# Mixing a chunk of 256 and one of 512 tokens, in place of three of 256, on each block of weights

## Chip, core and metric

The kernel runs on one core of a Trainium2 chip. The metric is the time of one execution on the device in microseconds, the median of several runs. TensorE does the matmuls, VectorE, ScalarE and GpSimd the rest, and SyncE (SP) issues most of the transfers.

## What is computed

Three layers follow each other: attention within clusters, a mixture of experts, and a bilinear layer. The change lies in the last, which the program calls the second stage:

```
def _moe2_ref(x, w_a, w_b, w_out) -> np.ndarray:
    a = x @ w_a
    b = x @ w_b
    return (a * b @ w_out).astype(np.float32)
```

x has 1536 tokens of 512 numbers. w_a and w_b are 512 x 1536, w_out is 1536 x 512. The weights come as 64-bit floats. The experts' outputs, which are x, go to a buffer ys_d in DRAM, sorted by expert, and come back from it in chunks of tokens.

## The kernel before

To hold its precision, the kernel splits each factor of a product into a high and a low part in the type fp32r, and makes a product of three matmuls (high by high, low by high, high by low). `mm3` issues these for a list of weight and token tiles: with four pieces of 128 rows (j = 0 to 3) that is 12 matmuls, first the two with the tokens' high part for each j, then those with the low part.

The second stage goes by steps I. One step has one chunk of tokens and one of 12 blocks of 128 columns of w_a and w_b. `bil1` multiplies the chunk by both blocks (24 matmuls), ScalarE copies the first result out of PSUM (L1311), VectorE multiplies it by the second (L1312), and ScalarE and VectorE split the product g into its two parts (L1313, L1317). `bil2` multiplies g by the block's rows of w_out, one or two steps later, and adds up in PSUM over the 12 blocks: three matmuls of 512 columns for each 128 tokens. At a chunk's end `leave` scales the sums by the gates and sends them out.

The order of steps is a list. Before, the first 36 steps mix three chunks of 256 tokens: on each four blocks of weights come four steps of chunk 0, four of chunk 1 and four of chunk 2. Then 12 steps take a chunk of 512 tokens and 12 a chunk of 256. A step of 256 tokens is called narrow here, one of 512 wide. A matmul of `bil1` has as many columns as the chunk has tokens.

While the first chunks are mixed, the weights of later blocks are still being loaded and narrowed from 64-bit floats, one piece of 128 x 512 in a step: `narrow_a` (ScalarE, L1053), `narrow_b` (VectorE, L1065 to L1067), `narrow_c` (ScalarE, L1073) and `narrow_d` (VectorE, L1079). The raw pieces stand in four buffers; the load of a piece four further on goes out when `narrow_b` is done with the buffer.

A chunk's tokens are loaded by `load_x2`, at the step that the table X2 gives, and split into high and low part by `split_x2` (ScalarE L1281, VectorE L1282), at the step that X2S gives. Steps below zero lie in the experts' stage. The outputs of the last expert, in the tile ys_7, are put into ys_d by `put_rows` (L1257) at step 2, behind that step's `load_x2`. The rows that it writes come from a register.

Engines take their instructions in the order in which the program issues them. Tiles that share a tag share its buffers: "xe" has two, which hold ys_6 and ys_7 when the second stage begins, and "xT" has two. The eight PSUM banks are sc0 to sc3, pp, pv, et0 and et1.

Of the kernel before, what the change touches and what calls it, by code (L numbers as in the profile page):

```python
# [9 lines left out]
F32 = mybir.dt.float32  # L10
F32R = mybir.dt.float32r
# [11 lines left out]
P = 128  # L23
FAR = float(2.0 ** 100)
CAP = 256
# [4 lines left out]
NA = 5  # L30
RAMP0, RAMP = 8, 3
GR = 5
CHUNKS = ((0, 256), (256, 256), (512, 256), (768, 512), (1280, 256))
X2 = {-7: 0, 0: 1, 4: 2, 27: 3, 39: 4}
X2S = {-3: [(0, 0), (0, 1)], 2: [(1, 0), (1, 1)], 6: [(2, 0), (2, 1)], 29: [(3, 0)], 31: [(3, 1)], 42: [(4, 0)], 43: [(4, 1)]}
I0 = 0
PACE = (1,)
YW = 1
CG0 = 2
LEAD = 24  # L40
# [7 lines left out]
def kernel(  # L48
# [15 lines left out]
    nc = tc.nc  # L64
# [12 lines left out]
    DC = DM // P  # L77
# [6 lines left out]
    rawp = ctx.enter_context(tc.tile_pool(name="rawp", bufs=NRAW))  # L84
# [13 lines left out]
    ys_v = ys_d.rearrange("(j p) n -> p j n", p=P)  # L98
# [21 lines left out]
    wide = w_a.dtype == I64  # L120
# [9 lines left out]
    raw = {}  # L130
    raw2 = {}
    hl = {}
# [675 lines left out]
    for s in range(nst):  # L808
        g_, h, t = steps[s]
        pp = g_[0]  # L810
# [149 lines left out]
    big = ctx.enter_context(tc.tile_pool(name="big", bufs=1, reuse_waits="tile"))  # L960
    xT_t = {}

    def new_x(key, dt=F32R):
        return big.tile([P, 2, DC, CAP], dt, tag="xT", name=f"xT_{key}", bufs=2)
# [82 lines left out]
    def narrow_a(m):  # L1047
        for _ in range(min(m, 4 * NCH - nsplit[0])):
            load_raw()
            w, hi, lo = open_part()  # L1050
            if w.dtype == I32:
                a = big.tile([P, 512], F32, tag="a", name=f"a_{nsplit[0]}", bufs=NA)
                nc.scalar.activation(a, w[:, :, 1].bitcast(F32), AF.Abs, scale=2.0 ** -112)  # L1053
                narrowed.append((w, a, hi, lo))
            else:
                nc.scalar.copy(hi, w)
                nc.gpsimd.tensor_sub(lo, w, hi)
            ndone[0] += 1
            load_raw()

    def narrow_b(m):
        for _ in range(min(m, len(narrowed))):
            w, a, hi, lo = narrowed.pop(0)
            low, top, au = w[:, :, 0].bitcast(U32), w[:, :, 1].bitcast(U32), a.bitcast(U32)
            nc.vector.tensor_scalar(out=au, in0=au, scalar1=3, scalar2=None, op0=ALU.logical_shift_left)  # L1065
            nc.vector.scalar_tensor_tensor(out=au, in0=low, scalar=29, in1=au, op0=ALU.logical_shift_right, op1=ALU.bitwise_or)
            nc.vector.scalar_tensor_tensor(out=au, in0=top, scalar=0x80000000, in1=au, op0=ALU.bitwise_and, op1=ALU.bitwise_or)  # L1067
            late.append((a, hi, lo))
# [7 lines left out]
    def narrow_d():  # L1076
        while lows:
            a, hi, lo = lows.pop(0)
            nc.vector.tensor_sub(lo, a, hi)  # L1079
# [34 lines left out]
    def mm3(ps, pairs):  # L1114

        ops = [o for (sh, sl_), (mh, ml) in pairs for o in ((sh, mh), (sl_, mh))]
        ops += [(sh, ml) for (sh, _), (_, ml) in pairs]
        for i, (s_, m_) in enumerate(ops):
            nc.tensor.matmul(ps, s_, m_, start=(i == 0), stop=(i == len(ops) - 1))  # L1119
# [51 lines left out]
    LAG = 2  # L1171
# [87 lines left out]

    NF2 = F2 // P  # L1260
    HD = DC // 2

    def load_x2(ck):

        at, wd = CHUNKS[ck]
        if ck == 2:
            x = [big.tile([P, DC, CAP], F32R, tag="xe", name=f"x2{n}_{ck}", bufs=2) for n in "hl"]
            x = [[x[m][:, HD * u:HD * u + HD] for u in range(2)] for m in range(2)]
        elif wd == CAP:
            x = new_x(f"b{ck}")  # L1270
            x = [[x[:, m, HD * u:HD * u + HD] for u in range(2)] for m in range(2)]
        else:
            x = [[rawp.tile([P, HD, wd], F32R, tag="raw", name=f"x2_{ck}{m}{u}") for u in range(2)] for m in range(2)]
        for u in range(2):
            nc.sync.dma_start(out=x[1][u].bitcast(F32), in_=ys_v[:, HD * u:HD * u + HD, at:at + wd])
        xT_t["b", ck] = x

    def split_x2(ck, u):

        hi, lo = (x[u] for x in xT_t["b", ck])  # L1280
        nc.scalar.copy(hi, lo.bitcast(F32))  # L1281
        nc.vector.tensor_sub(lo, lo.bitcast(F32), hi)  # L1282

# [1 line left out]
    outs = []  # L1285
    o_ps = {}
    o_f = {}
    banks = [("sc0", "sc1"), ("sc2", "sc3"), ("pp", "pv"), ("sc0", "sc1", "sc2", "sc3"), ("sc0", "sc1")]

    def bil1(I):  # L1290
        ck, f = order[I]
        c, ff = divmod(f, 4)
        at, wd = CHUNKS[ck]
        xh, xl = xT_t["b", ck]
        if wd == CAP:
            pab = ps_t.tile([P, 2, CAP], F32, tag=f"et{I % 2}", name=f"ab_{I}")
            pab = pab[:, 0, :], pab[:, 1, :]
        else:
            pab = [ps_t.tile([P, wd], F32, tag=t, name=f"ab{z}_{I}") for z, t in enumerate((("et0", "et1"), ("pp", "pv"))[I % 2])]
        for z in range(2):  # L1300
            w = hl[NCE + 3 * c + z]
            mm3(pab[z], [((w[:, 0, j, ff * P:(ff + 1) * P], w[:, 1, j, ff * P:(ff + 1) * P]), (xh[j // HD][:, j % HD, :], xl[j // HD][:, j % HD, :])) for j in range(DC)])
        narrow_a(PACE[I % len(PACE)] > 0 if I >= I0 else 0)
        if wd == CAP:
            ga = big.tile([P, CAP], F32, tag="ga", name=f"ga_{I}", bufs=2)
            g2 = big.tile([P, 2, CAP], F32R, tag="hh", name=f"g_{I}", bufs=4)
            gh, gl = g2[:, 0], g2[:, 1]
        else:
            ga = big.tile([P, wd], F32, tag="a", name=f"ga_{I}", bufs=NA)
            gh, gl = (big.tile([P, wd], F32R, tag="hh", name=f"g{m}_{I}", bufs=4) for m in range(2))  # L1310
        nc.scalar.copy(ga, pab[0])  # L1311
        nc.vector.tensor_mul(ga, pab[1], ga)  # L1312
        nc.scalar.copy(gh, ga)  # L1313
        narrow_c()
        narrow_a(PACE[I % len(PACE)] > 1 if I >= I0 else 0)
        narrow_b(1)
        nc.vector.tensor_sub(gl, ga, gh)  # L1317
        narrow_b(1)
        narrow_d()
        gs_[I] = (gh, gl)  # L1320

    def leave(ck, t):
# [32 lines left out]
                leave(ck, t)  # L1355


    order = [(ck, 4 * c + ff) for c in range(NF2 // 4) for ck in range(3) for ff in range(4)]
    order += [(ck, f) for ck in (3, 4) for f in range(NF2)]
    after = {J + LAG: [J] for J in range(len(order))}  # L1360
    w0 = 3 * NF2
    after.update({w0 + 1: [w0], w0: [w0 - 2, w0 - 1], w0 + NF2 + 1: []})
    after.update({J + 1: [J] for J in range(w0, w0 + NF2)})
    tot = len(order)
    pg_ = put_gates(lambda: gs_[max(gs_)][0])
    for G in range(total_f + tot + LAG):
        I = G - total_f

        skip_whole()
        room = 4 * (NSLOT + 2 * (max(G - LAG, 0) // 4)) - nsplit[0]  # L1370
        if 4 * NCE <= nsplit[0] and I < 0 and G % NF > 1:
            narrow_a(min(room, 1))
        if G == 1:
            ranks()
        if G == 2:
            limits()
        if G == GR:
            rare()
        if I < 0:
            layer1(G)  # L1380
            if G in (2, NF - 1):
                load_xe(1 if G == 2 else 2)
            if G == NF:
                further()
            if G == GR - 2:
                tc.mark_branch_hint_location("rare", "LikelyTaken", engines=[mybir.EngineType.DVE])
            e, f = divmod(G, NF)
            if 2 * NF <= G < 3 * NF:
                next(rr, None)
            if G > 3 * NF:  # L1390
                next(gg, None)
            if f == (5 if e else NF - 2):
                if e + 1 < NE:
                    trans_x(e + 1, xe_t[e + 1])
            if f == 5 and 0 < e < NE - 2:
                load_xe(e + 2)
        elif I < tot:
            bil1(I)
            next(pg_, None)
        if I in X2:  # L1400
            load_x2(X2[I])
        for ck, u in X2S.get(I, ()):
            split_x2(ck, u)
        if I >= LAG:
            for J in after[I]:
                bil2(J)
        elif G >= LAG:
            layer2(G - LAG)
        put_rows(G - LAG)
        if 3 <= G < total_f:  # L1410
            load_whole(G)
        if nsplit[0] < 4 * NCE:

            ramp = RAMP0 + 2 * min(G, GR - 2) + RAMP * max(G - GR + 1, 0)
            split_some(min(room, 2 * G + lead - nsplit[0], ramp - nsplit[0], 4 * NCE - nsplit[0]))
        elif I < 0:
            narrow_c()
            narrow_b(1)
            narrow_d()
        if G == GR - 1:  # L1420
            tc.mark_branch_hint_location("rare", "LikelyTaken", engines=[mybir.EngineType.SP])
# [30 lines left out]
```

## Time and profile before

| | |
|---|---|
| time, median of 3 runs | 779.07 us (778.71 to 779.94) |
| the profiled execution | 778.49 us |
| its span, first to last instruction | 776.4 us |
| TensorE busy | 754.8 us, 97% |
| VectorE busy | 462.6 us, 60% |
| ScalarE busy | 378.4 us, 49% |
| step 0 of the second stage begins | 464.67 us |
| the first wide step (step 36) begins | 617.44 us |
| the first step of the last chunk (step 48) begins | 716.30 us |

Times within an execution count from the first instruction of the span. A matmul's end is modelled and overlaps the next one's start, so a stretch of matmuls is measured from one start to another.

### The profile page before, as it was taken

The page shows a single profiled execution, that of the slowest core. Times are in us where ns is not written, and L with a number is a line of the kernel's source. Part 1 is how long each engine was busy: PE and PEld are TensorE (multiplying, and loading weights), DVE is VectorE, ACT ScalarE, POOL GpSimd, SP SyncE. Part 2 cuts the span into 40 slices and gives each one's busy share as a digit, 9 for nine tenths or more (in the row PEclk, how much of TensorE's full clock was granted, in tenths as well). Part 3 has the DMA queues.
Part 4 walks back from the last instruction along what each step waited for, and adds up shares of the span by engine and source line. Part 5 has one row for each costly group of instructions (what it writes and reads, how often), then busy time and mean ns, then how long its engine had stood idle before and what let it go on. Part 6 is the DMA issues. An engine that isn't in the chain of part 4 may idle for free.

```text
span 776.4 us, 13347 instructions
## 1 busy us (share of the span) xinstructions
PE 754.8 (97%) x5097; PEld 648.5 (84%) x5097; DVE 462.6 (60%) x929; ACT 378.4 (49%) x794; POOL 106.1 (14%) x143
## 2 busy tenths in 40 slices
PE   8899999999999988999999999999999999999996
PEld 5667777777777668999999999999999988888995
DVE  6776665787767776378876898877743221121211
ACT  5656766667675665266654555544423211111211
POOL 6203212051300041000000004420001110000201
PEclk9999999999999999999999999999999999999999
DMA  7228133152221026789879866773401000000100
GB/s 187 60 80 270 45 94 87 59 182 96 60 52 32 28 96 225 271 299 296 276 243 275 280 218 186 154 139 113 136 1 55 28 28 1 0 1 1 55 1 27
DMA packets 48519, 91.91 MB, mean 118 GB/s; under 512 B 6328, under 2 KB 21304, under 8 KB 48448
## 3 DMA queue, kind: packets, MB, share of 16 engines
q1 hardware_dynamic: 44240, 81.01, 35.8%
q0 software_dynamic: 2304, 6.31, 2.1%
q10 hardware_dynamic: 1904, 3.67, 1.3%
q8 instruction: 41, 0.67, 0.3%
q14 instruction: 30, 0.25, 0.1%
HBM read 69.27 MB, written 14.04 MB: 107 GB/s over the span
## 4 chain that ended last, share of the span: by engine, by line
PE 32%; issue 22%; DVE 2%; DMA 2%; POOL 1%; ACT 1%; POOLq 0%; DVEq 0%; ACTq 0%
PE ab L1119 11%; PE y L1236 4%; PE o_sc L1352 4%; PE h L1201 3%; PE y L1240 2%; PE h L1119 2%; PE h L1193 2%; DMA raw<-in_moe_w_dram 2%; PE h L1202 1%; DVE w L207 1%; PE y L1241 1%; POOL out_dram L1330 1%; PE o_pp L1352 1%; PE o_pv L1352 1%; PE xT L1100 0%
## 5 line engine op out<-in xcount | busy, mean ns | idle before, releaser
L1312 DVE TENSOR_TENSOR ga<-ab,ga 128x256 f32<-128x256 f32 (+1 forms) x60 | 28.6, 477 | 156.0 <-ACT ga L1311 84.8
L564 ACT ACTIVATE E<-sc,nmx 128x768 f32<-128x768 f32 x96 | 86.8, 904 | 56.3 <-DVE nmx L559 47.3
L1119 PEld LDWEIGHTS ab<-xT_b,w 128*128 128x128 f32 x864 | 107.8, 191 | 2.6
L1119 PE MATMUL ab<-xT_b,w 128*128 128x256 f32 x864 | 109.2, 283 | 0.0
L559 DVE TENSOR_REDUCE nmx<-sc 128x1 f32<-128x768 f32 x96 | 91.4, 953 | 17.1 <-PE sc L551 16.0
L1311 ACT COPY ga<-ab 128x256 f32<-128x256 f32 (+1 forms) x60 | 25.0, 417 | 151.9 <-PE ab L1119 151.9
L579 PEld LDWEIGHTS et<-ident,E 128*128 128x128 f32 x576 | 62.6, 141 | 34.7 <-ACT ET L583 12.5
L1352 PE MATMUL o_sc<-w,g 128*128 128x512 f32 x360 | 90.1, 392 | 0.0
L579 PE MATMUL et<-ident,E 128*128 128x128 f32 x576 | 82.2, 279 | 4.8 <-ACT E L564 2.8
L585 DVE COPY ET<-et 128x384 f32<-128x384 f32 x96 | 52.6, 548 | 54.9 <-PE et L579 54.8
L1352 PEld LDWEIGHTS o_sc<-w,g 128*128 128x128 f32 x360 | 65.4, 189 | 12.1
L606 PE MATMUL pv<-ET,v 128*64 128x384 f32 (+2 forms) x408 | 73.0, 479 | 0.6 <-ACT ET L583 0.5
L550 PE MATMUL sc<-K,Q 80*128 80x512 f32 x192 | 72.8, 380 | 0.5 <-DMA Q<-Q 0.5
L207 DVE TENSOR_TENSOR w<-raw,w 128x1024 fp32r<-128x1024 f32 x48 | 58.2, 1219 | 17.2 <-ACT w L206 16.6
L1119 PE MATMUL ab<-x,w 128*128 128x512 f32 x288 | 67.7, 391 | 0.2 <-DVE ot L1329 0.2
L1119 PEld LDWEIGHTS ab<-x,w 128*128 128x128 f32 x288 | 54.0, 188 | 12.1 <-DVE ot L1329 0.6
L551 PE MATMUL sc<-K,Q 128*128 128x512 f32 x192 | 61.7, 342 | 0.0
L1236 PE MATMUL y<-hh,w 128*128 128x256 f32 (+3 forms) x416 | 59.4, 290 | 0.8 <-issue 0.8
L206 ACT CAST w<-raw 128x1024 fp32r<-128x1024 f32 x48 | 50.3, 1051 | 16.1 <-DMA raw<-in_moe_w_dram 11.1
L1313 ACT CAST g<-ga 128x256 fp32r<-128x256 f32 (+1 forms) x60 | 26.9, 449 | 59.7 <-DVE ga L1312 59.7
L1236 PEld LDWEIGHTS y<-hh,w 128*128 128x128 f32 x416 | 54.5, 190 | 1.2 <-issue 0.9
L583 ACT COPY ET<-et 128x384 f32<-128x384 f32 x96 | 45.7, 476 | 2.7 <-PE et L579 2.6
(272 smaller groups left out, 1253.9 us busy)
## 6 DMA issues: line engine op xcount, KB each, us to landing
raw<-in_moe_w_dram SPq DMA_DIRECT2D x48, 512.0 KB, 5.1
w<-in_moe_w_dram SPq DMA_DIRECT2D x16, 512.0 KB, 6.6
raw<-in_moe_w_a_dram SPq DMA_DIRECT2D x12, 512.0 KB, 4.5
raw<-in_moe_w_b_dram SPq DMA_DIRECT2D x12, 512.0 KB, 4.8
raw<-in_moe_w_out_dram SPq DMA_DIRECT2D x12, 512.0 KB, 5.2
xs_d<-zero SPq DMA_DIRECT2D x8, 512.0 KB, 6.2
xe<-xs_d ACTq DMA_DIRECT2D x7, 512.0 KB, 7.2
v<-in_v_dram SPq DMA_DIRECT2D x8, 384.0 KB, 3.1
```

The costliest lines, as they stand in the source:

```text
L206: nc.scalar.copy(hi, w)
L207: nc.vector.tensor_sub(lo, w, hi)
L550: nc.tensor.matmul(ps[:, lo:hi], Q3[:, qs], K3[:, h * S + lo:h * S + hi], start=True, stop=False)
L551: nc.tensor.matmul(ps[:, lo:hi], Q2[:, qs], K2[:, h * S + lo:h * S + hi], start=False, stop=True)
L559: nc.vector.tensor_reduce(out=nmx[pp][:, h, t:t + 1], in_=sc[s], axis=AX.X, op=ALU.max, negate=True)
L564: nc.scalar.activation(e, sc.pop(s), AF.Exp, bias=nmx[pp][:, h, t:t + 1], accum_out=sums[pp][:, t, h:h + 1])
L579: nc.tensor.transpose(pt[:, j * P:(j + 1) * P], e[:, kt * P:(kt + 1) * P], ident)
L585: nc.vector.tensor_copy(dst, src)
L606: nc.tensor.matmul(pv[h * D:(h + 1) * D, :], vt[:, h, kt, :], ets[g, h][:, kt, :n * P], start=(kt == 0), stop=(kt == NT - 1))
L1119: nc.tensor.matmul(ps, s_, m_, start=(i == 0), stop=(i == len(ops) - 1))
L1236: nc.tensor.matmul(ys_ps[e][j // 2][:, j % 2, :wd], w[:, m_, ff, j * P:(j + 1) * P], s_, start=(f == 0 and i == 0 and j % 2 == 0), stop=(l ...
L1352: nc.tensor.matmul(o_ps[ck][t], s_[:, t * P:(t + 1) * P], w_[:, m_], start=(f == 0 and i == 0), stop=(J == I and f == NF2 - 1 and i == 2))
```

## The change

Chunks 1 and 2, of 256 tokens each, become one chunk of 512. The mixed part then has 24 steps: on each four blocks of weights four narrow steps of chunk 0 and four wide steps of chunk 1. The chunks behind it stay, under new numbers (2 and 3).

The 512 tokens of chunk 1 stand in two halves: j = 0, 1 in a tile of tag xT, j = 2, 3 in two tiles of tag xe. `load_x2` loads a half at a time, so X2 has entries for halves. A wide step narrows a second piece at its end. Wide steps have their results in et0 and et1 alone, where they had taken turns with pp and pv; chunk 0 adds up in pp and pv, chunk 1 in sc0 to sc3. When a step's `bil2` runs is worked out by a loop: after the next step for a wide one, two steps later for a narrow one.

```diff
-CHUNKS = ((0, 256), (256, 256), (512, 256), (768, 512), (1280, 256))
-X2 = {-7: 0, 0: 1, 4: 2, 27: 3, 39: 4}
-X2S = {-3: [(0, 0), (0, 1)], 2: [(1, 0), (1, 1)], 6: [(2, 0), (2, 1)], 29: [(3, 0)], 31: [(3, 1)], 42: [(4, 0)], 43: [(4, 1)]}
+CHUNKS = ((0, 256), (256, 512), (768, 512), (1280, 256))
+X2 = {-7: [(0, 0), (0, 1)], 0: [(1, 0)], 2: [(1, 1)], 19: [(2, 0), (2, 1)], 27: [(3, 0), (3, 1)]}
+X2S = {-3: [(0, 0), (0, 1)], 2: [(1, 0)], 3: [(1, 1)], 20: [(2, 0)], 21: [(2, 1)], 30: [(3, 0)], 31: [(3, 1)]}
...
-    def load_x2(ck):
+    x2_t = {}
+
+    def load_x2(ck, u):
 
         at, wd = CHUNKS[ck]
-        if ck == 2:
-            x = [big.tile([P, DC, CAP], F32R, tag="xe", name=f"x2{n}_{ck}", bufs=2) for n in "hl"]
-            x = [[x[m][:, HD * u:HD * u + HD] for u in range(2)] for m in range(2)]
-        elif wd == CAP:
-            x = new_x(f"b{ck}")
-            x = [[x[:, m, HD * u:HD * u + HD] for u in range(2)] for m in range(2)]
+        if wd == CAP:
+            if u == 0:
+                x2_t[ck] = new_x(f"b{ck}")
+            x = [x2_t[ck][:, m, HD * u:HD * u + HD] for m in range(2)]
+        elif ck == 1 and u == 0:
+            x = new_x("b1").rearrange("p m j n -> p m (j n)").rearrange("p m (j n) -> p m j n", n=wd)
+            x = [x[:, m] for m in range(2)]
+        elif ck == 1:
+            x = [big.tile([P, HD, wd], F32R, tag="xe", name=f"x2_{ck}{m}{u}", bufs=2) for m in range(2)]
         else:
-            x = [[rawp.tile([P, HD, wd], F32R, tag="raw", name=f"x2_{ck}{m}{u}") for u in range(2)] for m in range(2)]
-        for u in range(2):
-            nc.sync.dma_start(out=x[1][u].bitcast(F32), in_=ys_v[:, HD * u:HD * u + HD, at:at + wd])
-        xT_t["b", ck] = x
+            x = [rawp.tile([P, HD, wd], F32R, tag="raw", name=f"x2_{ck}{m}{u}") for m in range(2)]
+        nc.sync.dma_start(out=x[1].bitcast(F32), in_=ys_v[:, HD * u:HD * u + HD, at:at + wd])
+        xT_t["b", ck, u] = x
...
-    banks = [("sc0", "sc1"), ("sc2", "sc3"), ("pp", "pv"), ("sc0", "sc1", "sc2", "sc3"), ("sc0", "sc1")]
+    banks = [("pp", "pv"), ("sc0", "sc1", "sc2", "sc3"), ("sc0", "sc1", "sc2", "sc3"), ("pp", "pv")]
...
-            pab = [ps_t.tile([P, wd], F32, tag=t, name=f"ab{z}_{I}") for z, t in enumerate((("et0", "et1"), ("pp", "pv"))[I % 2])]
+            pab = [ps_t.tile([P, wd], F32, tag=f"et{z}", name=f"ab{z}_{I}") for z in range(2)]
...
         nc.vector.tensor_sub(gl, ga, gh)
-        narrow_b(1)
         narrow_d()
+        if wd > CAP:
+            narrow_a(1)
+            narrow_b(1)
...
-    order = [(ck, 4 * c + ff) for c in range(NF2 // 4) for ck in range(3) for ff in range(4)]
-    order += [(ck, f) for ck in (3, 4) for f in range(NF2)]
+    order = [(ck, 4 * c + ff) for c in range(NF2 // 4) for ck in range(2) for ff in range(4)]
+    order += [(ck, f) for ck in (2, 3) for f in range(NF2)]
...
+        lag = 1 if J < len(order) and wide[J] else LAG
+        after[J] = [K for K in todo2 if K <= J - (1 if wide[K] else lag)]
```

The SP queue around step 2, before. xT_b1 and x2l_2 are the tokens of chunks 1 and 2, raw_... the weights' pieces, and ys_7 is what `put_rows` writes:

```order
L1275 DMA xT_b1_7077<-ys_d_75 128x2x256 x2
L152 DMA raw_65_7111<-in_moe2_w_b_dram 128x1024
L152 DMA raw_66_7160<-in_moe2_w_b_dram 128x1024
L1256 TENSOR_LOAD ov_i_3500
L1256 ISA x2
L1257 REGISTER_ALU
L1257 DMA ys_d_75<-ys_7_7130 128x4x176
L152 DMA raw_67_7225<-in_moe2_w_b_dram 128x1024
L152 DMA raw_68_7274<-in_moe2_w_out_dram 128x1024
L1275 DMA x2l_2_7290<-ys_d_75 128x2x256 x2
```

The same place in the change, where x2_111 is the low tile of the second half of chunk 1 (the tile that the load writes):

```order
L1276 DMA xT_b1_7077<-ys_d_75 128x2x512
L150 DMA raw_65_7110<-in_moe2_w_b_dram 128x1024
L150 DMA raw_66_7159<-in_moe2_w_b_dram 128x1024
L1276 DMA x2_111_7175<-ys_d_75 128x2x512
L1254 TENSOR_LOAD ov_i_3500
L1254 ISA x2
L1255 REGISTER_ALU
L1255 DMA ys_d_75<-ys_7_7129 128x4x176
L150 DMA raw_67_7225<-in_moe2_w_b_dram 128x1024
```

The last load of tokens stood two loads of weights behind the put of ys_7, and now stands right ahead of it. In the built program the put waits for that load to land, since both touch ys_d.

ScalarE from step 3 on, before, where ab_3 and ab_4 are the results of steps 3 and 4:

```order
L1311 COPY ga_3_7227<-ab_3_7198 128x256
L1313 CAST g_3_7228<-ga_3_7227 128x256
L1073 CAST w_35_7059<-a_143_7158 128x512
L1053 ACTIVATE a_145_7272<-raw_64_7062 128x512
L1311 COPY ga_4_7276<-ab_4_7246 128x256
L1313 CAST g_4_7277<-ga_4_7276 128x256
```

And in the change, where x2_101 is the high tile of the second half of chunk 1 and ab0_4 the first result of the wide step 4:

```order
L1312 COPY ga_3_7227<-ab_3_7198 128x256
L1314 CAST g_3_7228<-ga_3_7227 128x256
L1071 CAST w_35_7059<-a_143_7157 128x512
L1282 CAST x2_101_7174<-x2_111_7175 128x1024
L1051 ACTIVATE a_145_7275<-raw_64_7062 128x512
L1312 COPY ga_4_7279<-ab0_4_7248 128x512
L1314 CAST g0_4_7280<-ga_4_7279 128x512
```

A split of tokens now stands between steps 3 and 4; before, the last one stood behind step 6. In the built program x2_101 has the address of ys_7, and the cast waits for the put of ys_7 to land.

TensorE at step 4, before:

```order
L1352 MATMUL o_0_sc0_7179<-w_34_6949,g_1_7114 128x512 x3
L1352 MATMUL o_0_sc1_7180<-w_34_6949,g_1_7114 128x512 x3
L1119 MATMUL ab_4_7246<-xT_b1_7077,w_32_6631 128x256 x12
L1119 MATMUL ab_4_7246<-xT_b1_7077,w_33_6789 128x256 x12
L1352 MATMUL o_0_sc0_7179<-w_34_6949,g_2_7163 128x512 x3
L1352 MATMUL o_0_sc1_7180<-w_34_6949,g_2_7163 128x512 x3
```

And in the change:

```order
L1354 MATMUL o_0_pv_7180<-w_34_6949,g_1_7113 128x512 x3
L1117 MATMUL ab0_4_7248<-xT_b1_7077,w_32_6631 128x512 x4
L1117 MATMUL ab0_4_7248<-x2_101_7174,w_32_6631 128x512 x4
L1117 MATMUL ab0_4_7248<-xT_b1_7077,w_32_6631 128x512 x2
L1117 MATMUL ab0_4_7248<-x2_111_7175,w_32_6631 128x512 x2
L1117 MATMUL ab1_4_7249<-xT_b1_7077,w_33_6789 128x512 x4
L1117 MATMUL ab1_4_7249<-x2_101_7174,w_33_6789 128x512 x4
L1117 MATMUL ab1_4_7249<-xT_b1_7077,w_33_6789 128x512 x2
L1117 MATMUL ab1_4_7249<-x2_111_7175,w_33_6789 128x512 x2
L1354 MATMUL o_0_pp_7179<-w_34_6949,g_2_7162 128x512 x3
L1354 MATMUL o_0_pv_7180<-w_34_6949,g_2_7162 128x512 x3
```

Step 4 reads chunk 1, whose second half it meets at its fifth matmul (x2_101) and its eleventh (x2_111).

## Rows read from the trace of the kernel before

**Rows 1.** The page's busy shares, and one stretch of the mixed part by windows.

```profile
PE 754.8 (97%) x5097; PEld 648.5 (84%) x5097; DVE 462.6 (60%) x929; ACT 378.4 (49%) x794; POOL 106.1 (14%) x143
...
core 0: us, PE busy (x) PEld busy (x) DVE busy (x) ACT busy (x) POOL busy (x), PEclk, DMA share, GB/s
475.00:500.00 25.00, 25.00 (x177) 23.45 (x177) 20.71 (x41) 13.37 (x28) 11.26 (x13) 1.00 0.72 160
```

**Rows 2.** TensorE in time, steps 3 and 4: start us, us, operation.

```profile
477.18 3.04 PE L1119 MATMUL ab<-xT_b,w 128*128 128x256 f32 x24
480.06 1.55 PE L1352 MATMUL o_sc<-w,g 128*128 128x512 f32 x6
481.44 3.04 PE L1119 MATMUL ab<-xT_b,w 128*128 128x256 f32 x24
```

**Rows 3.** TensorE in time, wide steps 36, 37 and 38, and step 48.

```profile
617.44 5.60 PE L1119 MATMUL ab<-x,w 128*128 128x512 f32 x24
...
625.94 5.78 PE L1119 MATMUL ab<-x,w 128*128 128x512 f32 x24 [0.18 <-DVE ot L1329]
...
634.27 5.60 PE L1119 MATMUL ab<-x,w 128*128 128x512 f32 x24
...
639.72 2.88 PE L1352 MATMUL o_sc<-w,g 128*128 128x512 f32 x12
...
716.30 3.04 PE L1119 MATMUL ab<-xT_b,w 128*128 128x256 f32 x24
```

**Rows 4.** Groups by form, 470 to 777 us: busy, mean ns, idle before.

```profile
L1079 DVE TENSOR_TENSOR w<-a,w 128x512 fp32r<-128x512 f32 x25 | 17.1, 685 | 0.1
L1067 DVE SCALAR_TENSOR_TENSOR a<-raw,a 128x512 uint32<-128x512 uint32 x24 | 16.6, 693 | 0.8
...
L1065 DVE TENSOR_SCALAR a<-a 128x512 uint32<-128x512 uint32 x23 | 9.6, 417 | 0.0
...
L1317 DVE TENSOR_TENSOR g<-ga,g 128x512 fp32r<-128x512 f32 x12 | 8.3, 693 | 8.2 <-ACT g L1313 8.2
...
L1282 DVE TENSOR_TENSOR x<-x,x 128x1024 fp32r<-128x1024 f32 x2 | 2.5, 1226 | 1.1 <-ACT x L1281 1.1
...
L1281 ACT CAST x<-x 128x1024 fp32r<-128x1024 f32 x2 | 2.1, 1044 | 0.0
```

**Rows 5.** SP in time, steps 1 to 4.

```profile
474.61 4.46 SPq L152 DMA_DIRECT2D raw<-in_moe_w_b_dram  x2
479.95 0.40 SPq L1257 DMA_DIRECT2D ys_d<-ys  x1
...
488.23 0.89 SPq L1275 DMA_DIRECT2D x2l<-ys_d  x2
```

**Rows 6.** DMA issues, whole span; the fourth from 478.0 to 479.5: KB, us to landing.

```profile
xT_b<-ys_d SPq DMA_DIRECT2D x6, 256.0 KB, 2.8
...
x<-ys_d SPq DMA_DIRECT2D x2, 512.0 KB, 3.7
...
ys_d<-ys SPq DMA_DIRECT2D x1, 496.0 KB, 6.4
...
raw<-in_moe_w_b_dram SPq DMA_DIRECT2D x1, 512.0 KB, 8.3
```

**Rows 7.** SP's own waits, 440 to 777 us: total us, times, longest.

```profile
SPq L1275 <- DMA ys_d<-ys: 0.6, 1, 0.6
```

**Rows 8.** TensorE's last matmuls, the last window, and the bf16 matmuls before and after 7.2 us.

```profile
765.91 4.27 PE L1352 MATMUL o_sc<-w,g 128*128 128x512 f32 x18
...
775.00:776.40 1.40, 0.00 (x0) 0.00 (x0) 0.00 (x0) 0.00 (x0) 0.00 (x0) 0.60 0.00 0
...
L261 PE MATMUL wps<-ones x8: 531/634/650, 3.5 to 7.0; 128*128 128x512 bf16 x8
...
L261 PE MATMUL wps<-ones x13: 379/379/531, 7.0 to 17.7; 128*128 128x512 bf16 x13
```

More of the change, by code (lines that the diff above doesn't have):

```diff
@@ L32 @@
 GR = 5
-CHUNKS = ((0, 256), (256, 256), (512, 256), (768, 512), (1280, 256))
-X2 = {-7: 0, 0: 1, 4: 2, 27: 3, 39: 4}
-X2S = {-3: [(0, 0), (0, 1)], 2: [(1, 0), (1, 1)], 6: [(2, 0), (2, 1)], 29: [(3, 0)], 31: [(3, 1)], 42: [(4, 0)], 43: [(4, 1)]}
-I0 = 0
-PACE = (1,)
+CHUNKS = ((0, 256), (256, 512), (768, 512), (1280, 256))
+X2 = {-7: [(0, 0), (0, 1)], 0: [(1, 0)], 2: [(1, 1)], 19: [(2, 0), (2, 1)], 27: [(3, 0), (3, 1)]}
+X2S = {-3: [(0, 0), (0, 1)], 2: [(1, 0)], 3: [(1, 1)], 20: [(2, 0)], 21: [(2, 1)], 30: [(3, 0)], 31: [(3, 1)]}
 YW = 1
@@ L1261 @@
     HD = DC // 2
-    def load_x2(ck):
+    x2_t = {}
+    def load_x2(ck, u):
         at, wd = CHUNKS[ck]
-        if ck == 2:
-            x = [big.tile([P, DC, CAP], F32R, tag="xe", name=f"x2{n}_{ck}", bufs=2) for n in "hl"]
-            x = [[x[m][:, HD * u:HD * u + HD] for u in range(2)] for m in range(2)]
-        elif wd == CAP:
-            x = new_x(f"b{ck}")
-            x = [[x[:, m, HD * u:HD * u + HD] for u in range(2)] for m in range(2)]
-        else:
-            x = [[rawp.tile([P, HD, wd], F32R, tag="raw", name=f"x2_{ck}{m}{u}") for u in range(2)] for m in range(2)]
-        for u in range(2):
-            nc.sync.dma_start(out=x[1][u].bitcast(F32), in_=ys_v[:, HD * u:HD * u + HD, at:at + wd])
-        xT_t["b", ck] = x
+        if wd == CAP:
[7 more added lines that the diff above has]
+            x = [big.tile([P, HD, wd], F32R, tag="xe", name=f"x2_{ck}{m}{u}", bufs=2) for m in range(2)]
+        else:
+            x = [rawp.tile([P, HD, wd], F32R, tag="raw", name=f"x2_{ck}{m}{u}") for m in range(2)]
+        nc.sync.dma_start(out=x[1].bitcast(F32), in_=ys_v[:, HD * u:HD * u + HD, at:at + wd])
+        xT_t["b", ck, u] = x
     def split_x2(ck, u):
-        hi, lo = (x[u] for x in xT_t["b", ck])
+        hi, lo = xT_t["b", ck, u]
         nc.scalar.copy(hi, lo.bitcast(F32))
@@ L1293, in bil1 @@
         at, wd = CHUNKS[ck]
-        xh, xl = xT_t["b", ck]
+        x = [xT_t["b", ck, u] for u in range(2)]
         if wd == CAP:
@@ L1298, in bil1 @@
         else:
-            pab = [ps_t.tile([P, wd], F32, tag=t, name=f"ab{z}_{I}") for z, t in enumerate((("et0", "et1"), ("pp", "pv"))[I % 2])]
+            pab = [ps_t.tile([P, wd], F32, tag=f"et{z}", name=f"ab{z}_{I}") for z in range(2)]
         for z in range(2):
             w = hl[NCE + 3 * c + z]
-            mm3(pab[z], [((w[:, 0, j, ff * P:(ff + 1) * P], w[:, 1, j, ff * P:(ff + 1) * P]), (xh[j // HD][:, j % HD, :], xl[j // HD][:, j % HD, :])) for j in range(DC)])
-        narrow_a(PACE[I % len(PACE)] > 0 if I >= I0 else 0)
+            mm3(pab[z], [((w[:, 0, j, ff * P:(ff + 1) * P], w[:, 1, j, ff * P:(ff + 1) * P]), (x[j // HD][0][:, j % HD, :], x[j // HD][1][:, j % HD, :])) for j in range(DC)])
+        narrow_a(1)
         if wd == CAP:
@@ L1314, in bil1 @@
         narrow_c()
-        narrow_a(PACE[I % len(PACE)] > 1 if I >= I0 else 0)
         narrow_b(1)
         nc.vector.tensor_sub(gl, ga, gh)
-        narrow_b(1)
         narrow_d()
+        if wd > CAP:
+            narrow_a(1)
+            narrow_b(1)
         gs_[I] = (gh, gl)
@@ L1355, in bil2 @@
                 leave(ck, t)
-    order = [(ck, 4 * c + ff) for c in range(NF2 // 4) for ck in range(3) for ff in range(4)]
-    order += [(ck, f) for ck in (3, 4) for f in range(NF2)]
[L1360 to L1363, printed above, removed]
+    order = [(ck, 4 * c + ff) for c in range(NF2 // 4) for ck in range(2) for ff in range(4)]
+    order += [(ck, f) for ck in (2, 3) for f in range(NF2)]
+    wide = [CHUNKS[ck][1] > CAP for ck, _ in order]
+    after = {}
+    todo2 = []
+    for J in range(len(order) + LAG):
+        if J < len(order):
+            todo2.append(J)
+        lag = 1 if J < len(order) and wide[J] else LAG
+        after[J] = [K for K in todo2 if K <= J - (1 if wide[K] else lag)]
+        todo2 = [K for K in todo2 if K not in after[J]]
     tot = len(order)
@@ L1399 @@
             next(pg_, None)
-        if I in X2:
-            load_x2(X2[I])
+        for ck, u in X2.get(I, ()):
+            load_x2(ck, u)
         for ck, u in X2S.get(I, ()):
```

## The prediction, made before the result was known

> **What bounds the kernel now.** I read the shares of the page first, then the stage's windows, then single engines in time. TensorE is busy 97% of the span, and in the stretch in which three chunks are mixed it is busy without a gap [rows 1]. So in this stage time is what TensorE's queue takes, and another engine counts only where TensorE would have to wait for it. The reader is to see in TensorE's timeline that step 3 begins at 477.18 and step 4 at 481.44: 24 matmuls of 256 columns in 2.88 us (120 ns each), then six of 512 in 1.38 us, 4.26 us in all [rows 2]. From step 3 to the first wide step at 617.44 there are 33 steps in 140.26 us, 4.25 us each [rows 2, 3]. In the wide stage 24 matmuls of 512 columns take 5.45 us (634.27 to 639.72, 227 ns each), and ten steps from 634.27 to 716.30 take 82.03 us, 8.20 us each [rows 3].
>
> **What merging gives.** A wide step takes the place of two narrow ones: 2 x 4.25 - 8.20 = 0.30 us. Twelve of them give 3.6 us. The bounds come from the slowest wide step shown (625.94 to 634.27, 8.33 us): 12 x 0.17 = 2.0 us, and from the narrow step of 4.26: 12 x 0.32 = 3.8 us. One small wait goes as well: before, step 37 starts 0.2 us late because its sums need a bank that the leaving chunk still holds [rows 3]; in the change wide sums stand in et0 and et1 only, and chunk 0's banks pp and pv are asked for again 18 steps later. Gain: 3.8 us.
>
> A page of the Trainium skill weighs against this: "TensorE: Matmul & The Clock Gate", section "Back-to-back issue gap", gives an isolated matmul at full clock as its columns over 2.4 GHz plus 2.5 ns, so that one of 512 columns saves 2.5 ns over two of 256; 288 pairs would give 0.7 us. The rows say 2 x 120 - 227 = 13 ns for a pair, five times as much, and I go by the rows.
>
> **The second piece in a wide step.** Two pieces are narrowed in each, at the old pace (one per 4.1 us). VectorE then does two each of L1065, L1066, L1067 and L1079, and L1312 and L1317 at 512 columns: 2 x (0.42 + 0.69 + 0.69 + 0.69) + 2 x 0.69 = 6.4 us of 8.20 [rows 4]; L1066 and L1312 are taken at what L1067 and L1317 show. The product must leave et1 before the next step's second half: it can start 5.5 us into a step, takes 0.69, and TensorE writes et1 again at 8.20 + 2.7 = 10.9 us. That is 4.7 us of cover, so I cost it at nothing; without the cover each wide step would pay in full. Raw pieces have four buffers, so a load is used two wide steps (16 us) after it goes out and lands within 8.3 us [rows 6]: nothing. The loads of chunks 2 and 3 move earlier, to where no load of weights is left behind them: nothing.
>
> **What the moved loads cost.** Chunk 1 is now 512 tokens, and its second half (j = 2, 3) loads at step 2, is split at step 3 and is read by the fifth matmul of step 4. Before, the last of the three loads went out at step 4, was split at step 6 and read at step 8. Here is a new chain, and each link stands in the order of the built program:
> - SP: the load of x2_111 comes behind raw_66 and *ahead* of the put of ys_7. The put writes rows of ys_d that are known only at run time, so it waits until the load of x2_111, which reads ys_d, has landed.
> - ScalarE: the copy into x2_101 (L1282) writes the memory that ys_7 stands in, so it waits until the put has landed.
> - TensorE: the fifth matmul of step 4 waits for that copy. All that follows on TensorE, the second sums of steps 2 and 3 too, stands behind it. VectorE stands behind its own subtraction (L1283), SP's raw_67 behind the put; raw_67 is wanted only late in step 5.
>
> Steps 0 to 3 are as before, so the clock times of before hold. The second of two raw loads is through SP at 474.61 + 4.46 = 479.07 [rows 5], so x2_111 goes out at about 479.2. Its price is that of 512 KB: 3.7 us where the queues were quiet, 8.3 us for the raw load just ahead of it at this very place [rows 6]. The put's price is from 2.8 us (a load of 256 KB; the put has 352 KB) to 8.3 us. The upper end is this put itself: it goes out at 479.95, and the load at 488.23 waited for it to land [rows 5, 7]. A put of 496 KB elsewhere took 6.4 us [rows 6]. I take the middle of each, 6.0 and 5.5 us, since neither end is clearly nearer: the queue is crowded at this place, but the put now goes out when the load has left it. The copy of 1024 columns takes 1.04 us [rows 4]. So 479.2 + 6.0 + 5.5 + 1.04 = 491.7. TensorE wants it at 481.44 + 4 x 0.227 = 482.35: **9.4 us of standstill**, with both ends low 4.4 us, with both high 14.5 us. The low half of the split (1.23 us on VectorE [rows 4]) is wanted six matmuls, 1.36 us, later, and is covered.
>
> **What the clock adds.** The granted clock is full everywhere but at the end: the last matmul ends at 770.18, and in 775.00 to 776.40 it is 0.60 on the mean, so it fell from 2.4 to 1.2 GHz in that idle time [rows 8]. A standstill of 9.4 us is longer than that idle time was, so I expect the fall here too. What getting back costs is read at the start: eight matmuls up to 7.2 us take 634 ns, the later ones 379: 8 x 0.255 = 2.0 us [rows 8]. I take 2.0; the other end is nothing, if the clock holds. The Trainium skill's page "TensorE: Matmul & The Clock Gate", Part 1, has the half rate as the idle state that activity releases; no row here shows it inside a kernel's run. Without it the sum would be 2.0 us lower.
>
> **Sum**, against the profiled execution's span of 776.4 us: - 3.6 - 0.2 + 9.4 + 2.0 = + 7.6, so 784.0 us of span, 786.1 us for that execution (778.49), and 786.7 us beside the median of 779.07, which lies 0.6 us above it.
>
> **Rivals.**
> 1. *The second half comes in time* and the change only gives: 779.07 - 3.8 = 775.3 us, faster. For it: in before no split is seen to wait for a transfer, and the new chain itself is in no row. It decides only if load, put and copy are through by 482.35 + 3.8, 6.9 us after 479.2; the shortest rows give 3.7 + 2.8 + 1.04 = 7.5 us. 6 in 100.
> 2. *A short standstill*: both transfers near their low ends, 4.4 us, and a clock that holds: - 3.8 + 4.4 = + 0.6, 779.7 us, no change that can be told (0.2%, 1.6 us, is about what a measurement of this kernel can tell). Against it: this put took 8.3 us. 3 in 100.
> 3. *VectorE sets the pace of wide steps.* If its 6.4 us grew past 8.20, each wide step would stretch; at 9.2 us twelve would cost 12 us more: 798.7 us. Against it: 4.7 us of cover, and no row in which its operations stretch. 3 in 100.
> 4. *A matmul costs by its columns alone*, so merging saves nothing: + 9.4 + 2.0 - 0.2 = + 11.2, 790.3 us. Against it: 227 ns against 2 x 120. (The page's formula above would give 789.6 us.) 3 in 100.
>
> The forecast holds the other 85. It has both unknown transfers in it. With one of them at an end and the other in its middle it goes from + 4.9 (put at 2.8) to + 10.4 us (put at 8.3); the gain's bounds add up to 1.6 us and the clock takes off up to 2.0. That makes 781 to 792 us, which also holds rival 4. Chances: faster 0.06, the same 0.03, slower 0.91.
>
> **What the changed profile would show.** TensorE idle once, before the fifth matmul of step 4, at about 482.4, for some 9 us, put down to ScalarE's L1282; ScalarE idle before L1282, put down to the DMA of ys_7; SP's put waiting for the load of x2_111. Then matmuls of 512 columns nearly twice as long for some us, and a granted clock below 1 in that window. After that narrow steps of 4.25 and wide ones of 8.20 us, with ScalarE and VectorE never the releaser, and the last matmul about 7.6 us later than 770.18. I am wrong if TensorE has no gap at step 4 (rival 1), if the load lands in under 4 us and the put in under 3 (rival 2), if gaps stand before the second half of every wide step (rival 3), or if wide steps in the mixed blocks take 8.5 us (rival 4).

## The result and the profile after

The changed kernel takes 788.5 us (785.38 to 790.36, 4 runs) against 778.89 us (777.78 to 779.94, 4 runs, the three of the table above and one more) for the kernel before on the same chip: ratio 1.0113, 95% interval 1.0094 to 1.0132. It is slower by 9.6 us, inside the predicted range and 1.8 us above the predicted 786.7. The profiled execution takes 789.17 us, its span 787.1.

TensorE in time, from step 3 to the first undisturbed wide step (start us, us, operation; in brackets the idle time before it and its releaser), and then the first steps of chunks 2 and 3. These answer to [rows 2, 3]:

```profile
480.02 3.04 PE L1117 MATMUL ab<-xT_b,w 128*128 128x256 f32 x24
...
484.29 1.07 PE L1117 MATMUL ab<-xT_b,w 128*128 128x512 f32 x4
494.73 2.08 PE L1117 MATMUL ab<-x,w 128*128 128x512 f32 x4 [9.37 <-ACT x L1282]
...
501.94 0.84 PE L1354 MATMUL o_pp<-w,g 128*128 128x512 f32 x3
...
504.66 1.07 PE L1117 MATMUL ab<-xT_b,w 128*128 128x512 f32 x4
...
512.82 1.07 PE L1117 MATMUL ab<-xT_b,w 128*128 128x512 f32 x4
...
628.78 5.60 PE L1117 MATMUL ab<-x,w 128*128 128x512 f32 x24
...
636.94 5.60 PE L1117 MATMUL ab<-x,w 128*128 128x512 f32 x24
...
727.12 3.04 PE L1117 MATMUL ab<-xT_b,w 128*128 128x256 f32 x24
```

Step 4, the first wide one, stops after its four matmuls on the first half. The fifth, wanted at 484.29 + 4 x 0.227 = 485.20, starts at 494.73, 9.53 us late. The 20 matmuls that are then left of the step take 7.21 us (494.73 to 501.94), where 20 x 0.227 = 4.54 would do: another 2.67 us. From then on TensorE has no wait any more up to the end of the kernel. A wide step takes 8.16 us (504.66 to 512.82), and 8.27 on the second four blocks of weights, as in the kernel before.

Who held it: ScalarE's casts and SP's transfers in time, then SP's own waits between 480 and 500 us (total us, times, longest), and the landing of the load that goes out at 481.95 (KB, us):

```profile
480.59 1.05 ACT L1282 CAST xT_b<-xT_b 128x1024 fp32r<-128x1024 f32 x1
493.63 1.04 ACT L1282 CAST x<-x 128x1024 fp32r<-128x1024 f32 x1 [8.68 <-DMA ys_d<-ys]
```

```profile
477.45 4.45 SPq L150 DMA_DIRECT2D raw<-in_moe_w_b_dram  x2
481.95 0.43 SPq L1276 DMA_DIRECT2D x<-ys_d  x1
489.43 0.40 SPq L1255 DMA_DIRECT2D ys_d<-ys  x1
490.26 0.34 SPq L150 DMA_DIRECT2D raw<-in_moe_w_b_dram  x1
```

```profile
SPq L1255 <- DMA x<-ys_d: 6.2, 1, 6.2
```

```profile
x<-ys_d SPq DMA_DIRECT2D x1, 512.0 KB, 7.5
```

Read from the last line back to the first, this is the chain of the prediction. The load of the second half goes out at 481.95, behind the raw piece, and lands 7.5 us later. The put of ys_7 stood in SP's queue for 6.2 us and goes out as the load lands, at 489.43. ScalarE's cast, which writes into ys_7's memory, starts at 493.63, so the put took some 4.1 us. The cast takes 1.04 us, and TensorE goes on at 494.73.

The granted clock, by windows (columns as in [rows 1]: busy times of the five engines, PEclk, DMA share, GB/s):

```profile
485.00:490.00 5.00, 0.35 (x2) 0.00 (x0) 1.67 (x4) 0.00 (x0) 1.47 (x2) 1.00 0.42 152
490.00:492.00 2.00, 0.00 (x0) 0.00 (x0) 0.00 (x0) 0.00 (x0) 0.00 (x0) 0.50 0.83 236
...
498.00:500.00 2.00, 2.00 (x6) 1.53 (x5) 0.00 (x0) 0.59 (x1) 0.00 (x0) 0.50 0.00 0
500.00:502.00 2.00, 2.00 (x10) 1.66 (x9) 0.00 (x0) 0.00 (x0) 0.00 (x0) 0.95 0.00 0
502.00:510.00 8.00, 8.00 (x37) 6.63 (x36) 5.33 (x9) 2.87 (x5) 1.71 (x2) 1.00 0.34 70
```

TensorE has been idle since about 485.4. The clock is full up to 490 and half (1.2 GHz) from then on, and it stays half while TensorE works again, from 494.73 to about 500.

**Where the time is.** From the start of step 3 to that of the last chunk it was 239.12 us before [rows 2, 3] and is 727.12 - 480.02 = 247.10 now: + 7.98. That is 9.53 late + 2.67 slow - a gain of 4.22. The span grew by 10.7, because step 3 already began 2.84 us later in this execution. That part lies ahead of the change: step 0 begins 2.84 us later too (467.51 against 464.67), and 1.72 us of it stand already at the first matmuls of the experts (295.69 against 293.97). In the traces of the nine kernels of this study step 3 begins between 476.48 and 480.26; what makes the difference was not followed. So kernels are compared below by this stretch as well as by their times.

### The profile page after: what moved, and what is told of

It reads as the page before. It is cut to its first block, busy times and chain, and to the rows that moved or that the text cites. A ratio compares the mean times of both kernels' runs of the same rounds, so it can differ in the third digit from the quotient of the medians.

```text
span 787.1 us, 12726 instructions
## 1 busy us (share of the span) xinstructions
PE 755.3 (96%) x4809; PEld 636.9 (81%) x4809; DVE 459.4 (58%) x903; ACT 374.8 (48%) x768; POOL 105.3 (13%) x143
## 4 chain that ended last, share of the span: by engine, by line
issue 28%; PE 23%; DMA 5%; DVE 2%; POOL 1%; ACT 1%; SPq 0%; POOLq 0%; ACTq 0%; DVEq 0%
PE ab L1117 6%; PE y L1234 4%; PE h L1199 3%; PE y L1238 2%; PE h L1117 2%; DMA ys_d<-ys 2%; DMA raw<-in_moe_w_dram 2%; PE o_sc L1354 1%; PE h L1191 1%; PE h L1200 1%; PE y L1239 1%; DMA x<-ys_d 1%; POOL out_dram L1332 1%; DVE w L205 1%; DMA res<-tab_d 0%
## 5 line engine op out<-in xcount | busy, mean ns | idle before, releaser
L1313 DVE TENSOR_TENSOR ga<-ab,ga 128x256 f32<-128x256 f32 (+1 forms) x48 | 26.8, 558 | 160.6 <-PE ab L1117 114.3
L1117 PE MATMUL ab<-x,w 128*128 128x512 f32 x432 | 109.7, 394 | 9.4 <-ACT x L1282 9.4
L1117 PE MATMUL ab<-xT_b,w 128*128 128x256 f32 (+1 forms) x720 | 114.4, 306 | 0.0
L1117 PEld LDWEIGHTS ab<-xT_b,w 128*128 128x128 f32 x720 | 99.4, 192 | 7.5
L1117 PEld LDWEIGHTS ab<-x,w 128*128 128x128 f32 x432 | 82.0, 190 | 27.3 <-ACT x L1282 9.8
L1312 ACT COPY ga<-ab 128x256 f32<-128x256 f32 (+1 forms) x48 | 23.1, 481 | 129.9 <-PE ab L1117 126.8
L1354 PE MATMUL o_sc<-w,g 128*128 128x512 f32 x288 | 69.5, 390 | 0.0
L1314 ACT CAST g<-ga 128x256 fp32r<-128x256 f32 (+1 forms) x48 | 24.7, 514 | 84.5 <-DVE ga L1313 84.5
L1354 PEld LDWEIGHTS o_sc<-w,g 128*128 128x128 f32 x288 | 53.9, 188 | 11.3
L204 ACT CAST w<-raw 128x1024 fp32r<-128x1024 f32 x48 | 50.2, 1051 | 17.8 <-DMA raw<-in_moe_w_dram 12.8
```

The source lines that it names most:

```text
L1354: nc.tensor.matmul(o_ps[ck][t], s_[:, t * P:(t + 1) * P], w_[:, m_], start=(f == 0 and i == 0), stop=(J == I and f == NF2 - 1 and i == 2))
```

## The experiments

The stated theory is that two transfers in series, load and put, then the cast, hold TensorE, and that the clock's fall comes from the standstill. Rivals: one of the transfers alone holds it; the order of the two on SP is what costs; the slow matmuls are something of wide steps and not of idle time. In the first two and the sixth kernel added lines move line numbers by 10 (L1282 is L1292).

**1. The put out of the chain.** The last expert's rows go into two tiles of tag "a" and are put from there by two transfers. The cast of the second half then writes memory that no put reads. One of the two puts goes out at 481.51, 1.25 us behind the load; the other still waits on SP until the load has landed (5.1 us).

```diff
+            if e == NE - 1:
+                yts = [big.tile([P, 2, CAP], F32, tag="a", name=f"ys_{e}{u}", bufs=NA) for u in range(2)]
+                for u in range(2):
+                    (nc.vector.tensor_copy if u else nc.scalar.copy)(yts[u][:, :, :wd], ys_ps[e][u][:, :, :wd])
...
+                for u in range(2):
+                    nc.sync.dma_start(out=ys_v[:, 2 * u:2 * u + 2, bass.ds(row, WIDTHS[e])], in_=yts[u][:, :, :WIDTHS[e]])
```

> The last expert's outputs stand in two tiles of another tag, so the copy into x2_101 no longer waits for their put; loads and splits stay at steps 2 and 3. Theory (load and put stand in series in the standstill): the standstill of the change, 9.4 us, loses the put's 4.1 us, so TensorE stands for about 5 us at step 4, released by the copy, which waits for the load; whether the clock falls is open, so 1 to 4 us above the kernel before (780 to 783). Rival (the load alone sets it, the put only lies beside it): the standstill stays near 9 us and the time near 788.

Measured: 784.49 us, ratio 1.007 (1.0056 to 1.0085). The cast and TensorE in time, and the load's landing:

```profile
489.34 1.04 ACT L1292 CAST x<-x 128x1024 fp32r<-128x1024 f32 x1 [6.09 <-DMA x<-ys_d]
490.44 2.08 PE L1117 MATMUL ab<-x,w 128*128 128x512 f32 x4 [6.73 <-ACT x L1292]
```

```profile
x<-ys_d SPq DMA_DIRECT2D x1, 512.0 KB, 9.0
```

With the put gone from the chain the standstill is 6.73 us, and its last wait is the cast's for the load: the load makes it without the put. It falls by 2.6 and not by the put's 4.1 because the load itself took 9.0 us here. So the standstill and the time are both above what was expected (about 5 us, 780 to 783).

**2. The load early as well.** To the first kernel's edit:

```diff
-X2 = {-7: [(0, 0), (0, 1)], 0: [(1, 0)], 2: [(1, 1)], 19: [(2, 0), (2, 1)], 27: [(3, 0), (3, 1)]}
+X2 = {-7: [(0, 0), (0, 1)], 0: [(1, 0), (1, 1)], 19: [(2, 0), (2, 1)], 27: [(3, 0), (3, 1)]}
```

> As e1_put_off_chain, and the second half of chunk 1 is loaded at step 0, beside the first. Theory: no standstill is left, TensorE is busy through step 4, the clock stays full, and what is left is the gain of merging, 4 us: 774 to 776, a ratio of 0.995 to the kernel before. Rival (wide steps in the mixed part cost something of their own, by one pair of accumulators or by two pieces narrowed in each): 778 or more, with gaps inside the wide steps.

Measured: 776.97 us, ratio 0.9965 (0.9952 to 0.9979), faster than the kernel before, though 1 us above the range that was expected. With neither transfer in the way what is left is small, and it is the split:

```profile
486.13 1.19 PE L1117 MATMUL ab<-x,w 128*128 128x512 f32 x4 [0.54 <-ACT x L1292]
487.16 0.63 PE L1117 MATMUL ab<-xT_b,w 128*128 128x512 f32 x2
488.08 0.73 PE L1117 MATMUL ab<-x,w 128*128 128x512 f32 x2 [0.29 <-DVE x L1293]
```

**3. The put ahead of the load.** In the changed kernel, the other order on SP:

```diff
+        if I == 2:
+            put_rows(G - LAG)
         for ck, u in X2.get(I, ()):
             load_x2(ck, u)
```

> Only the order at step 2 is turned round: the put of ys_7 goes out first and the load of x2_111 behind it. Theory (two transfers in series, whichever leads): the load now waits for the put, because both touch ys_d, and the copy waits for the load; the standstill is again the sum of both, 8 to 12 us, and the time 786 to 791. Rival (only the put's place behind the load is at fault): the standstill falls to 5 us or less and the time to 783 or less.

Measured: 790.04 us, ratio 1.0126 (1.0108 to 1.0143). The standstill grows to 12.89 us, ended by the cast, and the cast now waits for the load. The put goes out at 480.33 and takes 10.5 us; the load goes out as it lands (490.80) and takes about 3.9:

```profile
494.81 1.04 ACT L1282 CAST x<-x 128x1024 fp32r<-128x1024 f32 x1 [12.20 <-DMA x<-ys_d]
495.91 2.08 PE L1117 MATMUL ab<-x,w 128*128 128x512 f32 x4 [12.89 <-ACT x L1282]
```

```profile
ys_d<-ys SPq DMA_DIRECT2D x1, 352.0 KB, 10.5
```

So the order is not what costs. The two stay in series either way, since both touch ys_d, and the one that goes out first, at about 480 behind two loads of weights, is slow (10.5 us here, 7.5 for the load in the changed kernel). Why it is slow there was not taken apart.

**4. Other work in the standstill.** In the changed kernel 32 matmuls on data that is there stand ahead of step 4. Their result is overwritten.

```diff
+            if I == 4 and z == 0:
+                for _ in range(32):
+                    nc.tensor.matmul(pab[1], w[:, 0, 0, :P], x[0][0][:, 0, :], start=True, stop=True)
```

> The change, with 32 matmuls of 512 columns ahead of step 4 whose results are overwritten: 7.3 us of work in the 9.4 us of standstill. Theory (the clock's fall costs 2.7 us on top of the standstill): the granted clock stays full, the matmuls behind the gap run at 227 ns, and the time is 2 to 3 us below the change (785 to 786.5 against 788.5). Rival (the standstill alone counts): the time is that of the change within 0.5 us.

Measured: 786.67 us, ratio 1.0085 (1.0069 to 1.0101). The matmuls take 7.25 us and leave 3.58 us idle. The clock did not hold, which was not expected, and the time lies just above the expected 785 to 786.5. TensorE in time, and the granted clock by windows:

```profile
482.27 7.42 PE L1305 MATMUL ab<-xT_b,w 128*128 128x512 f32 x32
489.52 1.07 PE L1117 MATMUL ab<-xT_b,w 128*128 128x512 f32 x4
494.17 1.57 PE L1117 MATMUL ab<-x,w 128*128 128x512 f32 x4 [3.58 <-ACT x L1282]
...
500.46 0.84 PE L1357 MATMUL o_pp<-w,g 128*128 128x512 f32 x3
```

```profile
492.00:494.00 2.00, 0.00 (x0) 0.00 (x0) 0.00 (x0) 0.93 (x1) 0.00 (x0) 1.00 0.50 104
494.00:496.00 2.00, 1.83 (x6) 1.45 (x7) 1.22 (x1) 0.69 (x2) 0.00 (x0) 0.70 0.00 0
496.00:498.00 2.00, 2.00 (x6) 1.61 (x5) 0.00 (x0) 0.51 (x1) 0.00 (x0) 0.50 0.00 0
```

It is full through the idle time and falls within 1 us of TensorE's working again: in windows of 0.5 us it is 1.00 up to 494.5 and 0.50 from 495.0 on. The 20 matmuls take 6.29 us (494.17 to 500.46), 1.75 too much. This left open whether idle time is the cause, and the seventh kernel was made for it.

**5. The load early, the put in the chain.** The second kernel's line alone, in the changed kernel: ys_7 in one tile of tag "xe" as there.

> The chain with one link taken out: the load of the second half goes out in step 0, and the rows of the last expert are put as in the changed kernel, from one tile whose place the high half takes. Theory (the chain is load, then put, then cast, and each link's own time stands in it): the load lands some 6 us after it goes out in step 0, about where step 3 begins, so that the put goes out there and only its own 4.1 to 10.5 us and the cast (1.04) stand ahead of TensorE's fifth matmul of step 4, which is wanted some 4.3 us after step 3 begins; a standstill of 1 to 7 us stays, and with the clock's 0 to 2.7 the time is 777 to 785 us. Rival (the put alone holds TensorE, the load doesn't count): as the changed kernel, 787 us or more, with a standstill of 9 us. Other rival (the load alone counts): no standstill, 776 to 777.

Measured: 785.1 us, ratio 1.0067 (1.0049 to 1.0085). The load is through in time (SP's list of waits has none for it); the put goes out at 479.24 and the cast starts as it lands:

```profile
479.24 0.40 SPq L1255 DMA_DIRECT2D ys_d<-ys  x1
```

```profile
487.57 1.04 ACT L1282 CAST x<-x 128x1024 fp32r<-128x1024 f32 x1 [6.17 <-DMA ys_d<-ys]
488.67 2.07 PE L1117 MATMUL ab<-x,w 128*128 128x512 f32 x4 [6.87 <-ACT x L1282]
```

The standstill is 6.87 us, so the put makes one without the load as well: it took some 8.2 us, where it took 4.1 in the changed kernel. As in the first kernel, the link that was left took longer than in the changed kernel. Taking out the load, which had taken 7.5 us there, saves 3.6 us by the ratios (1.0067 against 1.0113); taking out the put in the first kernel saves 3.4 us, which is not told apart from the put's 4.1. The execution in the trace, 782.16 us, is the quickest of the six; two of 785.9 us and one of 786.4 have a lower mean clock (0.989 to 0.991 against 0.995), so their standstill may have been longer.

**6. The second half split one step earlier.** The second kernel, with the split of (1, 1) in step 2:

```diff
-X2S = {-3: [(0, 0), (0, 1)], 2: [(1, 0)], 3: [(1, 1)], 20: [(2, 0)], 21: [(2, 1)], 30: [(3, 0)], 31: [(3, 1)]}
+X2S = {-3: [(0, 0), (0, 1)], 2: [(1, 0), (1, 1)], 20: [(2, 0)], 21: [(2, 1)], 30: [(3, 0)], 31: [(3, 1)]}
```

> Both links taken out as in the run with the early load, and the second half split in step 2, in place of step 3. Theory: the two gaps of TensorE left in that run (0.54 and 0.29 us, behind ScalarE's cast and VectorE's subtraction of the second half) go, and nothing is late in their place, so that the stretch from step 3 to the last chunk is 235.1 to 235.6 us and the time about 775.5 to 776.2, a ratio to before near 0.995. Rival (ScalarE and VectorE have no room for it in step 2, and the same wait comes up one step earlier): 776.5 to 778.

Measured: 775.55 us, ratio 0.9947 (0.9931 to 0.9963), the fastest kernel of the study. One window, 480 to 500 us, shows no idle time of TensorE and a full clock:

```profile
480.00:500.00 20.00, 20.00 (x94) 16.70 (x93) 14.76 (x25) 9.29 (x17) 5.64 (x7) 1.00 0.51 126
```

**7. More work in the standstill.** The fourth kernel with 46 matmuls in place of 32.

> The changed kernel with 46 matmuls on data that is there already (their result is overwritten) in front of step 4, in place of 32: some 10.4 us of work in the place of the standstill. Theory (the clock's loss is a matter of TensorE standing idle): idle left is under 1.5 us, the granted clock stays 1.00 through step 4 and behind it, and the time is the changed kernel's less its 2.7 us of slow matmuls: 785 to 787 with a stretch from step 3 to the last chunk of 244 to 246 us. Rival (the clock falls there whatever TensorE does): slow matmuls again, 248 us or more, and a time like the changed kernel's or longer.

Measured: 786.5 us, ratio 1.0082 (1.0066 to 1.0098). TensorE in time, and two windows:

```profile
483.64 10.59 PE L1305 MATMUL ab<-xT_b,w 128*128 128x512 f32 x46
494.06 1.07 PE L1117 MATMUL ab<-xT_b,w 128*128 128x512 f32 x4
495.31 1.20 PE L1117 MATMUL ab<-x,w 128*128 128x512 f32 x4 [0.17 <-ACT x L1282]
```

```profile
484.00:494.00 10.00, 10.00 (x46) 8.29 (x45) 2.02 (x4) 0.30 (x1) 1.82 (x2) 1.00 0.62 181
494.00:498.00 4.00, 3.83 (x17) 2.83 (x17) 1.23 (x1) 2.18 (x3) 0.00 (x0) 1.00 0.02 9
```

The second half is as late as ever, but TensorE is not idle, the clock stays full and the 20 matmuls take 4.66 us. So the slow matmuls come from the idle time. The Trainium skill's page "TensorE: Matmul & The Clock Gate", Part 1, has the half rate as an idle state that activity releases; the changed kernel (9.37 us idle, clock 0.50) and this one (0.17 us idle, clock 1.00) agree with it.

**All of them in one sum.** Us, from the starts in the traces: the fifth matmul of step 4 against its due time (start of the step + 0.91), inserted work, the 20 matmuls after it above 4.54, and the stretch from step 3 to the last chunk against 239.12. What is left is the gain.

| kernel | late | inserted | slow | stretch | gain |
|---|---|---|---|---|---|
| changed | 9.53 | 0 | 2.67 | + 7.98 | 4.22 |
| 1 | 6.88 | 0 | 2.01 | + 4.67 | 4.22 |
| 2 | 0.70 | 0 | 0.70 | - 2.82 | 4.22 |
| 3 | 13.05 | 0 | 2.57 | + 11.39 | 4.23 |
| 4 | 3.74 | 7.25 | 1.75 | + 8.52 | 4.22 |
| 5 | 7.02 | 0 | 1.70 | + 4.50 | 4.22 |
| 6 | 0.00 | 0 | 0.00 | - 4.24 | 4.24 |
| 7 | 0.34 | 10.42 | 0.12 | + 6.66 | 4.22 |

(In kernels 2 and 7 the clock is full. Their slow column holds what matmuls behind a wait take longer even so: four take 1.03 us, 486.13 to 487.16 and 495.31 to 496.34, where 0.91 would do. In kernel 2 it holds a second gap besides.) The gain is the same in all eight, so these three columns hold all that differs between them in this stretch.

## Why the prediction was right

- **Merging** was put at 3.6 + 0.2; it gives 4.22. From step 3 to the first step of chunk 2 it was 140.26 us [rows 2, 3] and is 628.78 - 480.02 = 148.76; less the 12.20 of the wait and the slow matmuls (9.53 + 2.67) that is 136.56, a gain of 3.70: the 3.6 of the sum. The rest, 0.52, lies in the 12 steps of chunk 2 (98.86 us before [rows 3], 727.12 - 628.78 = 98.34 now) and was put at 0.2. The bank wait was worth more than its 0.18 of idle time: steps 36 and 37 took 8.50 and 8.33 us before [rows 3], and the same two steps take 8.16 each now (628.78 to 636.94 and on). By the Trainium skill's page "TensorE: Matmul & The Clock Gate", section "Back-to-back issue gap", with its formula for an isolated matmul, a pair would have saved 2.5 ns; the trace has 3.70 us / 288 = 12.8 ns. Rival 4 falls.
- **The second piece** was put at nothing, hidden behind TensorE. No wait of TensorE stands in the changed trace behind step 4, and VectorE is busy 5.33 and 5.94 us in the two wide steps from 504.66, below the 6.4 that were reckoned. Rival 3 falls, and the loads of chunks 2 and 3 cost nothing.
- **The chain** was put at 9.4 us of standstill. From the time at which the fifth matmul was due it is 9.53 (9.37 of idle time), by the links that were named. The agreement of the total owes something to chance: the load took 7.5 us and not 6.0, the put 4.1 and not 5.5, and the two errors cancel. Both lie within the bounds of [rows 5, 6]. Rivals 1 and 2 fall: the second half doesn't come in time, nor nearly.
- **The clock** was put at 2.0 and cost 2.67. This term was too small by a third of itself. What was short is the number of slow matmuls and not the price of one: the first 12 of the 20 take 5.28 us (494.73 to 500.01), 0.21 us more than 0.227 each, and the last eight 0.11 us too much in all; the sum had eight at 0.255. That it came so near is in part luck, since [rows 8] don't show that the eight matmuls at the kernel's start ran at the slower clock. The windows of the kernel before grant the full clock there:

```profile
4.00:6.00 2.00, 2.00 (x9) 0.93 (x7) 1.97 (x8) 0.95 (x3) 2.00 (x11) 1.00 0.64 181
6.00:7.00 1.00, 1.00 (x6) 0.45 (x5) 0.73 (x4) 1.00 (x3) 0.30 (x2) 1.00 0.00 0
```

- **The sum**: - 4.22 + 9.53 + 2.67 = + 7.98 in the stretch, against + 7.6. The medians differ by 9.6. The kernel before has medians of 779.86 and 779.69 (11 runs each) beside the later kernels, which would make it 8.7. What is left, 0.7 to 1.6 us, is within what step 3's start and the transfers differ from one execution to another; it was not followed further.

What decides is thus one wait and not the merge: the same merge with its second half at hand (kernel 6) is faster than the kernel before by 4.1 us, as its gain of 4.24 has it. Rival 1 put that case 3.8 us below the kernel before.

## What to carry to other kernels

When chunks are merged, the first step that reads the larger chunk moves forward, and its loads must move with it: follow each new load through its queue and through the memory that it takes over, as far as the engine that sets the time. If two transfers stand in series through a buffer and a DRAM tile, taking one out of the chain may give less than its time, and swapping them may give nothing; here both had to go. A standstill of the bounding engine can cost a slower clock behind it beside its own length (1.70 to 2.67 us here), which is worth a term of its own.

## What was not expected of the hardware

- The same transfers take very different times within a few us of each other. The put of ys_7 (352 KB) took 4.1 to 4.6 us where it went out at 488.6 to 489.6, with the DMA engines nearly idle just before (a share of 0.03 from 488 to 490 in the changed kernel) and a raw piece 0.8 us behind it. It took 8.2 to 10.5 us where it went out at 479 to 480, right behind two raw pieces. The load of 512 KB took 3.9 us behind the put in kernel 3, and 7.5 to 9.0 us at 480 to 482, behind two raw pieces. Which other transfer of that moment makes it so was not taken apart.
- In kernel 4 the clock was full through 3.58 us without work and fell as work resumed, and cost 1.75 us. In the changed kernel, with an idle time 2.6 times as long, it cost 2.67. In kernels 1, 5 and 3 idle times of 6.73, 6.87 and 12.89 us cost 2.01, 1.70 and 2.57. So the loss does not grow with the standstill, and a short one is not cheap in proportion.
